# More units of the block-product scheme with tokens on partitions, in a fused attention and mixture-of-experts kernel

## The chip, the cores and the metric

One core of one Trainium2 chip. The metric is the device time of one execution in microseconds; times before and after are medians over runs. The engines are named as the profile names them: PE is TensorE's matmul, PEld its weight load, DVE is VectorE, ACT ScalarE, POOL GpSimd (here it mostly issues loads), SP SyncE, whose queue issues the DMA transposes, the small loads and the stores.

## The reference

Attention with a sliding window of 128 positions and 4 sink positions over 4 batches, 8 heads, 768 tokens and a head size of 64, then a mixture of 4 experts over the 3072 tokens that it gives, where each row is the 8 heads side by side (512 values):

```python
scores = scale * np.matmul(q, k.transpose(0, 1, 3, 2))
keep = is_sink | in_window          # k < n_sink, or 0 <= q - k < window
a = exp(where(keep, scores, -1e9) - max); a = a / sum(a)
x = (a @ v).transpose(0, 2, 1, 3).reshape(3072, 512)
p = domain_probs / domain_probs.sum(-1)
for e in range(4):
    h = np.maximum(x @ w1[e], 0.0)          # 512 -> 1024
    out += p[:, e:e + 1] * (h @ w2[e])      # 1024 -> 512
```

Only matmul inputs are bf16; sums are fp32.

## The kernel before

**Pairs and units.** The tokens are worked in pairs (b, g): batch b, two tiles of 128 tokens (256 tokens), so three pairs to a batch and twelve in all. A unit (b, g, e) is one pair and one expert: its *first products* make the hidden values H (x times w1, ReLU, gate), its *second products* turn H into output rows.

**Two ways of first products.** A plain unit runs 32 matmuls of 256 columns (L1118). A fast unit replaces the 2 by 2 block product by seven products of half the size, P1 to P7 (run in the order P1, P5, P6, P2, P7, P3, P4), over formed sums of the weights and of the tokens. Seven eighths of the columns are left. `START` says from which pair on an expert's units are fast.

**Two ways of fast units.** `emit_fast` (L1208) has F, the hidden index, on partitions: 56 matmuls of 128 columns, 8 to a product, into PSUM tiles `cps`; VectorE does ReLU and gate in one instruction (L1241), with gates spread over all partitions in a tile that a DMA fills (L478). `emit_turning` (L1320), a *turned* unit, has tokens on partitions: 14 matmuls of 512 columns, two to a product, and here a gate is one number per partition (`own_gates`). So the unit's values come out the wrong way round and are turned by two DMA transposes on SP's queue. The steps, in the order of a unit:

- P1: if the PSUM bank of tile Y was not wholly written by such a unit before, a clearing product of 512 columns; ScalarE copies X to Y (seed).
- P5: ScalarE copies it (L1373, `keep`) into `c5`, which is the memory of half-tile X[1], read as fp32.
- P6: VectorE adds c5 and X into V (L1367, `both`); P7 and P3 accumulate onto this.
- P7: VectorE adds into c5 (L1382). P4 ends the unit.
- Gates: ReLU (L1338) and then a scale (L1341) on ScalarE, or both in one on VectorE (L1345), into the bf16 half-tiles X[0] and X[1]; when both halves of one are in, SP issues its transpose into H[:, k] (L1301).

**Half-tiles.** A turned unit opens only when two half-tiles are free. They are not its own: `self.resting` is a list of (time, tile) that starts empty and is filled with memory that other stages have done with (the gate tiles after the last gated unit, three tiles of `qkn` after batch 3 is transposed, later `onat` and `aT`). After its transpose a half-tile goes back to the list. Which unit may be turned is set by `OWN` (the first batch with `own_gates`) and `TURNED_UNITS`; before, all units from batch 2 on but the first four are turned, 20 in all.

```python
def halves(self):
    return sum(x[0] <= t["pe"] + REST for x in self.resting)
```

The planned time at which a half-tile comes back is the end of its transpose on the planner's clock plus `LANDS`.

**Second products** are also in seven products (L1493), with weight forms and with sums S of H made by VectorE (L1434), but for the pairs (0, 0) and (0, 1), which run plain (L1579) and add expert by expert (`emit_second`).

**Attention.** Loads of q, k, v by POOL (L251 `qkn`, L318 `vx`), transposes of q and k by SP (L263 `qkT`), scores (L708, and the sinks' scores L669) on TensorE, exp on ScalarE (L733), a 0/1 mask on VectorE (L727; batch 0 L742; the first group of batch 0 is masked by a matmul that adds a bias), sums and values (L767, L774), reciprocal R (L801), scaling into `onat` (L819 ACT, L812 and L804 DVE), transposes into `xT` (L791), from which the first products read. w1 and w2 of each expert are loaded by POOL (L331, L341).

**What sets the order.** All instructions are emitted once by a planner in Python. It keeps a clock for each engine; `later(engine, ready, slack, run)` puts work for VectorE or ScalarE on a list, which `flush` empties by due time. The main loop picks the next step of TensorE among attention, first products, products of the second stage and plain second products, by the time at which each is ready and by a priority (`DUE`, `LOW_PRODUCT`, `LOW_SECOND`, `SHARE_OF`, `LEAD` and so on). Each engine then runs its list in this order and waits on semaphores where the data is not there. `EXPERTS` gives the order of experts within a pair. `gates_by_row` and `load_gates` fetch the gate tiles, `NGATE` halves of them in a ring. `own_load` and `own_made` fetch and normalise `own_gates` (four small VectorE steps).

Of the kernel before, what the change touches and what calls it, by code (L numbers as in the profile page):

```python
# [16 lines left out]
def kernel(  # L17
# [12 lines left out]
    nc = tc.nc  # L30
# [33 lines left out]
    EXPERTS = {(1, 0): (0, 2, 1, 3), (1, 1): (3, 2, 1, 0), (1, 2): (3, 2, 1, 0), (2, 2): (2, 0, 3, 1), (3, 1): (3, 2, 1, 0)}  # L64
    FIRST = 1
    START = {0: (1, 0), 1: (0, 2), 2: (0, 0), 3: (1, 0)}
    MIX = 6
    SHARE_OF = (1.01, 0.92, 0.96)
    LEAD = (1.01, 0.99)
    DUE = 1.9  # L70
    LOW_PRODUCT = 2.9
    LOW_SECOND = 2.7
    HIGH_PRODUCT = 1.9
    EARLY = -0.01
    MASK = 5000
    GATE = 800
    GATE0 = 300
    FORM = 6000
    TOKEN = 3000
    MARGIN = 500  # L80
    HOLD = 0
    FULL = 7
    STEP0 = 0.03
# [8 lines left out]
    OPEN = 2.5  # L92
    SOON = 34000
    NEARLY = 2
# [5 lines left out]
    ONE = 2  # L100
    HOLDS = 2
    MORE = 2
    BOTH = 1
    PAIR = 0
    OVER = 4
    ALONE = 2.0
    BEHIND = 1500
    CHORES = 3
    BIASED = 1
# [19 lines left out]
    def act(cols, *deps):  # L129
        at = max([t["act"], *deps])  # L130
        t["act"] = at + max(196, 68 + cols / 1.23)
        return at + max(350, 205 + cols / 1.2)

    def dve(cols, *deps, rate=0.96, fixed=157):
        at = max([t["dve"], *deps])
        t["dve"] = at + fixed - 85 + cols / rate
        return at + fixed + 35 + cols / rate

# [23 lines left out]
    def later(engine, ready, slack, run):  # L162

        pend.append((ready, ready + slack, engine, run))
# [294 lines left out]

    gate_sb = {}  # L460
    gate_tiles = [consts.tile([P, 2, 2, P], FP32, name=f"gates{i}") for i in range(NGATE // 2)]
# [21 lines left out]

# [26 lines left out]
    for tb in (2, 3):  # L510
# [18 lines left out]
    LOW = 32768.0  # L529
    low = [lent[:, 5 * P:8 * P], lent[:, 8 * P:12 * P]]  # L530
    nc.vector.tensor_scalar(
        out=low[0].rearrange("p (n q) -> p n q", n=3)[:, 0::2], in0=two, scalar1=LOW, scalar2=-LOW, op0=ALU.mult, op1=ALU.add,
    )
    nc.vector.tensor_scalar(out=low[0][:, P:2 * P], in0=own, scalar1=-LOW, scalar2=None, op0=ALU.mult)
    nc.vector.memset(low[0][0:NSINK, 0:2 * P], 0.0)
# [3 lines left out]
    x = low[1].rearrange("p (n c q) -> p n c q", n=2, c=2)  # L539
    nc.scalar.activation(out=x[:, :, 0], in_=two, func=AF.Copy, scale=-LOW)  # L540
    nc.scalar.activation(out=x[:, :, 1], in_=two, func=AF.Copy, scale=LOW, bias=-LOW)
    mask0 = consts.tile([P, 3 * P], BF16, name="mask0")
    mask1 = consts.tile([P, 4 * P], BF16, name="mask1")
    made = []

    def make_mask(i):
        def run(engine):
            x = (mask0, mask1)[i]
            if i:
                nc.scalar.activation(out=x, in_=low[i], func=AF.Copy, scale=1 / LOW, bias=1.0)  # L550
                act(4 * P)
            else:
                nc.vector.tensor_scalar(out=x, in0=low[i], scalar1=1 / LOW, scalar2=1.0, op0=ALU.mult, op1=ALU.add)
                dve(3 * P)
            made.append(i)
        later(("dve", "act")[i], (24000.0, 11700.0)[i], 8000, run)
# [132 lines left out]
    def scores(b, hp, g, more=False):  # L689
# [10 lines left out]
        if biased:  # L700
            for ph in range(2):
                nc.tensor.matmul(sps[ph][:, 0:w], lhsT=ident, rhs=low[min(g, 1)], start=True, stop=False, skip_group_check=True)
            pe(2 * w, ready, n=2)
# [18 lines left out]
        if b == 0:  # L722
            part = join(2, masked)
        else:
            def mask_both(at):
                def run(engine):
                    nc.vector.tensor_mul(a, a, m[:, None, :].to_broadcast([P, 2, w]))  # L727
                    masked(dve(2 * w, rate=1.92))
                later("dve", at, MASK, run)
            part = join(2, mask_both)  # L730
        for ph in range(2):
            def run(engine, ph=ph):
                nc.scalar.activation(out=a[:, ph], in_=sps[ph][:, 0:w], func=AF.Exp, scale=scale)  # L733
                at = act(w)
                take(slots[ph], at)
                if b or biased:
                    part(at)
                    return
                assert 1 in made

                def mask_one(engine):
                    nc.vector.tensor_mul(a[:, ph], a[:, ph], m)  # L742
# [217 lines left out]
    class Mixture:  # L960


        def __init__(self):
# [61 lines left out]
        def opened(self, b, g, e):  # L1025
# [58 lines left out]
        def emit_first(self, what, ready):  # L1084
# [56 lines left out]
            def run(engine):  # L1141
# [5 lines left out]
                part(at)  # L1147
            later("dve", end, GATE0, run)

# [32 lines left out]
        def emit_fast(self, u, m, ready):  # L1182
# [40 lines left out]
            def gated(dst, src, half_, ready, slack, slot=None, then=None):  # L1223
# [16 lines left out]
                def run(engine):  # L1240
# [5 lines left out]
                    if then:  # L1246
                        then(at)
                later("dve", ready, slack, run)

# [35 lines left out]
        def emit_turning(self, u, m, ready):  # L1285
# [47 lines left out]
            def gated(k, s, src, ready, slack, slot=None, then=None):  # L1333
                gate = own_gates[:, 2 * ((b - OWN) * NG + g) + s, e:e + 1]

                def run(engine):
                    if engine == "act":
                        nc.scalar.activation(out=src, in_=src, func=AF.Relu)  # L1338

                        def scaled(engine):  # L1340
                            nc.scalar.mul(X[k][:, :, s], src, gate)  # L1341
                            done(act(n))
# [3 lines left out]
                    done(dve(n, fixed=OWNED_READ))  # L1346

# [218 lines left out]
        def emit_second(self):  # L1566
# [20 lines left out]
            def run(engine):  # L1587
                if e == 0:
                    nc.vector.tensor_scalar(out=dst, in0=op, scalar1=sc, scalar2=None, op0=ALU.mult)
                else:  # L1590
                    nc.vector.scalar_tensor_tensor(
                        out=dst, in0=op, scalar=sc, in1=dst, op0=ALU.mult, op1=ALU.add,
                    )
# [43 lines left out]
    work = [sum(NFB * NDB * G * (1 if (b, g) < START[e] else 7 / 8) + NFB * NDB * G * (1 if (b, g) < PAIRS[0] else 7 / 8) for g in range(NG) for e in range(E)) for b in range(B)]  # L1637
    ahead, upto, loaded, wide, rowed = 0, 0.0, 0, 0, 0
    asked = []
# [22 lines left out]
    while mix.more() or att.more():  # L1662
# [31 lines left out]
        if turns and (ahead < 2 or not mix.second) and landed.get(("qk", *turns[0]), 1e12) < now and (turns[0][0] <= ahead or turns[0][0] == ahead + 1 and not att.todo):  # L1694
# [17 lines left out]
        if ahead + 1 < B and not att.more() and (ahead == 0 or (ahead + 1, 0) in turned_at) and (ahead == 0 or mix.done >= sum(work[:ahead]) * LEAD[ahead - 1]):  # L1712
            ahead += 1
            if ahead == 1:
                own_load()
            elif ahead == 2:
                own_made()
            att = Attention(ahead)
# [79 lines left out]
```

## Time and profile before

| what | value |
|---|---|
| median of 3 runs | 353.89 us (353.55 to 354.12) |
| span of the profiled execution | 351.9 us |
| PE matmuls L1208 (fast, F on partitions) | 1120 in 20 units |
| PE matmuls L1320 (turned) | 280 in 20 units |
| PE matmuls L1118 (plain) | 256 in 8 units |
| DVE gate L1241 | 72 (54 from cps, 18 from H), 683 ns each |
| ACT ReLU L1338 / scale L1341 | 44 of 585 ns / 37 of 693 ns |
| gate loads L478 on SP | 20 of 128 KB |
| granted TensorE clock | 9 tenths or more in every one of 40 slices |
| POOL busy | 71.6 us, all of it in the first 200 us |

The busy time of PE is the sum over its instructions in the trace; the share in brackets is of the span. PEld, the weight load, overlaps PE. A matmul's own duration in the groups (273 ns for 256 columns) is longer than the spacing of two in a row, since they are pipelined: prices are better read as spacings, and the chain of waits gives these where many of one kind stand in a row. The timeline gives start, duration, engine, line, operation and, in brackets, how long the instruction waited and for whom.

### The profile page before, as it was taken

To read this page: it belongs to the slowest core of one execution; us is meant where nothing else is said; L and a number is where in the kernel's file an instruction comes from. 1 tells how busy PE (TensorE), PEld (TensorE's weight loads), DVE (VectorE), ACT (ScalarE), POOL (GpSimd) and SP (SyncE) were. 2 spreads that over 40 slices of the span, in tenths; PEclk is the share of its full clock that TensorE was granted. 3 is DMA by queue.
4 is the path that set the end of the run, shared out by engine and by line. 5 is a ranking of instruction groups with operands and counts; after the bars stand their busy time and mean duration, and the time that the engine had idled before them with its cause. 6 is when DMAs were issued, how large, how long until landed. Compare 5 with 4: busy or idle time off the path is not lost.

```text
span 351.9 us, 9351 instructions
## 1 busy us (share of the span) xinstructions
PE 346.2 (98%) x3721; PEld 266.0 (76%) x3721; DVE 282.8 (80%) x672; ACT 208.3 (59%) x476; POOL 71.6 (20%) x89
## 2 busy tenths in 40 slices
PE   8999999999999999999999999999999999999996
PEld 3685769656789998998999886755856676666685
DVE  5886999878999999799898999578768586675740
ACT  6863624447874443647453539689589767666611
POOL 8946114330546206100152000000000000000000
PEclk9999999999999999999999999999999999999999
DMA  9999999999999999920999602545437733545441
GB/s 178 178 188 195 223 214 181 179 160 174 162 147 165 121 145 122 132 64 9 109 173 159 113 32 62 120 101 120 80 91 174 127 89 93 120 120 115 67 120 61
DMA packets 161032, 45.61 MB, mean 130 GB/s; under 512 B 144740, under 2 KB 156996, under 8 KB 160988
## 3 DMA queue, kind: packets, MB, share of 16 engines
q0 software_dynamic: 79104, 17.31, 56.4%
q1 hardware_dynamic: 80828, 27.18, 40.1%
q8 instruction: 29, 0.48, 0.5%
q10 hardware_dynamic: 1056, 0.52, 0.5%
q14 instruction: 15, 0.12, 0.1%
HBM read 38.39 MB, written 6.34 MB: 127 GB/s over the span
## 4 chain that ended last, share of the span: by engine, by line
PE 75%; DMA 19%; POOL 5%; issue 1%; ACT 0%; POOLq 0%; SPq 0%
PE acc L1493 35%; PE cps L1320 17%; PE cps L1208 15%; DMA w<-in_moe_w_dram 12%; DMA qkn<-in_k_dram 4%; DMA qkT<-qkn 3%; PE sps L708 3%; PE od L774 2%; POOL qkn L251 2%; POOL w L331 1%; POOL vx L318 1%; PE hps L1118 1%; PE od L767 1%; POOL w L341 0%; PE acc L1579 0%
## 5 line engine op out<-in xcount | busy, mean ns | idle before, releaser
L1493 PEld LDWEIGHTS <-H 128*128 128x128 bf16 x708 | 66.5, 98 | 17.9 <-issue 1.1
L1493 PE MATMUL acc<-w,H 128*128 128x256 bf16 x420 | 56.9, 273 | 0.0
L733 ACT ACTIVATE aT<-sps 128x512 bf16<-128x512 f32 (+1 forms) x96 | 47.2, 579 | 16.3 <-PE sps L708 16.2
L1208 PEld LDWEIGHTS <-w 128*128 128x128 bf16 x640 | 39.1, 98 | 1.2 <-issue 0.5
L1493 PEld LDWEIGHTS <-S 128*128 128x128 bf16 x320 | 30.3, 98 | 9.5 <-issue 0.8
L1241 DVE SCALAR_TENSOR_TENSOR H<-cps,gates 128x512 bf16<-128x512 f32 x54 | 36.6, 683 | 0.0
L1338 ACT ACTIVATE cps<-cps 128x512 f32<-128x512 f32 x44 | 25.5, 585 | 17.5 <-PE cps L1320 17.0
L1118 PE MATMUL hps<-xT,w 128*128 128x256 bf16 x256 | 31.9, 273 | 0.1
L819 ACT ACTIVATE onat<-od,R 128x64 bf16<-128x64 f32 x108 | 24.9, 324 | 11.4 <-DVE R L801 11.1
L318 POOL DMA_DIRECT2D vx<-in_v_dram x24 | 21.4, 903 | 43.0 <-PE od L774 31.2
L1208 PEld LDWEIGHTS <-vf 128*128 128x128 bf16 x480 | 29.3, 98 | 1.0 <-issue 0.5
L1579 PE MATMUL acc<-w,H 128*128 128x512 bf16 x128 | 29.9, 379 | 0.0
L1493 PE MATMUL acc<-wf,H 128*128 128x256 bf16 (+1 forms) x216 | 29.6, 272 | 0.0
L1118 PEld LDWEIGHTS <-w 128*128 128x128 bf16 x256 | 24.1, 98 | 4.7 <-issue 0.9
L1341 ACT ACTIVATE rest<-cps,own_gates 128x512 bf16<-128x512 f32 x37 | 25.5, 693 | 0.7
L727 DVE TENSOR_TENSOR aT<-aT,mask 128x1024 bf16<-128x1024 bf16 (+1 forms) x36 | 22.7, 640 | 3.1 <-ACT aT L733 2.8
L251 POOL DMA_DIRECT2D qkn<-in_q_dram x22 | 19.7, 896 | 23.3 <-DMA qkT<-qkn 14.7
L1208 PE MATMUL cps<-T,w 128*128 128x128 bf16 x320 | 24.3, 219 | 0.0
L1208 PE MATMUL cps<-xT,w 128*128 128x128 bf16 x320 | 24.1, 219 | 0.0
L1320 PE MATMUL cps<-w,T 128*128 128x512 bf16 x80 | 23.8, 379 | 0.0
L1320 PE MATMUL cps<-vf,T 128*128 128x512 bf16 x80 | 23.6, 379 | 0.0
L1554 ACT COPY osb<-acc 128x256 f32<-128x256 f32 x32 | 12.1, 382 | 19.3 <-PE acc L1493 19.1
(145 smaller groups left out, 673.5 us busy)
## 6 DMA issues: line engine op xcount, KB each, us to landing
w<-in_moe_w_dram POOLq DMA_DIRECT2D x6, 1024.0 KB, 18.4
out_dram<-osb SPq DMA_DIRECT2D x16, 256.0 KB
vx<-in_v_dram POOLq DMA_DIRECT2D x24, 128.0 KB, 6.5
qkn<-in_q_dram POOLq DMA_DIRECT2D x22, 128.0 KB, 6.7
qkn<-in_k_dram POOLq DMA_DIRECT2D x22, 128.0 KB, 7.4
gates<-gate_rows SPq DMA_DIRECT2D x20, 128.0 KB
w<-in_moe_w_dram POOLq DMA_DIRECT2D x4, 256.0 KB, 6.9
w<-in_moe_w_dram POOLq DMA_DIRECT2D x2, 512.0 KB, 11.5
```

The lines of the kernel that those rows point to most:

```text
L251: nc.gpsimd.dma_start(out=both[:, i], in_=src[b, :, tb * P:(tb + 1) * P, :].rearrange("h p d -> p h d"),)
L318: nc.gpsimd.dma_start(out=vx[tb][:, :, 0:D], in_=v[b, :, tb * P:(tb + 1) * P, :].rearrange("h p d -> p h d"),)
L733: nc.scalar.activation(out=a[:, ph], in_=sps[ph][:, 0:w], func=AF.Exp, scale=scale)
L819: nc.scalar.mul(o[:, qi, hp, ph * D:(ph + 1) * D], od[:, qi, ph, 0:D], R[:, qi, ph])
L1118: nc.tensor.matmul(h[:, i].rearrange("p (q n) -> p q n", q=2), lhsT=w1_sb[e][:, db, fb * P:(fb + 1) * P], rhs=xT[b, g][:, :, db], start=(i ...
L1208: nc.tensor.matmul(y[:, f], lhsT=A[:, d, f * P:(f + 1) * P], rhs=T[:, d], start=(m in ("P1", "P5") and f == 0 and d == 0), stop=(d == 1), ...
L1241: nc.vector.scalar_tensor_tensor(out=dst, in0=src, scalar=0.0, in1=gate, op0=ALU.max, op1=ALU.mult)
L1320: nc.tensor.matmul(y.rearrange("p f n -> p (f n)"), lhsT=T[:, d], rhs=A[:, d], start=(m in ("P1", "P5") and d == 0), stop=(d == 1), skip_g ...
L1338: nc.scalar.activation(out=src, in_=src, func=AF.Relu)
L1341: nc.scalar.mul(X[k][:, :, s], src, gate)
L1493: nc.tensor.matmul(y, lhsT=self.operand(b, g, e, m)[:, f], rhs=forms[e][m][:, f, cs], start=(k == 0 and f == 0 and m in (("P1", "P5", "P2" ...
L1579: nc.tensor.matmul(op, lhsT=H[:, fb // QF, fb % QF, s], rhs=w2_sb[e][:, fb, :], start=(fb == 0), stop=(fb == NFB - 1),)
```

## The change

Sizes and switches:

```diff
-        [(0, 0, 2), (1, 1, 1)],
+        [(1, 1, 1), (0, 0, 2)],
...
-    NGATE = 4
+    NGATE = 2
     TURN_ABOUT = 1
-    OWN = 2
-    TURNED_UNITS = (4, 0)
-    EXPERTS = {(1, 0): (0, 2, 1, 3), (1, 1): (3, 2, 1, 0), ...}
+    OWN = 1
+    TURNED_UNITS = (1, 0, 1, 0, 0, 1, 1, 0, 1, 1, 1, 0, 1, 1, 1, 0, 1, 1, 1, 1, 1, 1, 0, 1, 1, 1, 1, 1, 1, 1, 1, 1, 1, 1, 1, 1)
+    EXPERTS = {(1, 0): (0, 2, 3, 1), (1, 1): (0, 3, 2, 1), ...}
...
-    START = {0: (1, 0), 1: (0, 2), 2: (0, 0), 3: (1, 0)}
+    START = {0: (1, 0), 1: (0, 2), 2: (0, 0), 3: (0, 2)}
...
-    REST = 3000
-    LANDS = 0
-    SCALED = 300
+    REST = 4000
+    LANDS = -1400
+    SCALED = 1100
...
-    OWNED_READ = 152
+    OWNED_READ = 218
+    OWNS = 9000
+    HALVES = 2
+    GATE_LANDS = 600
```

`TURNED_UNITS` is now one 0 or 1 for each unit from batch `OWN` on, in the order in which units are opened: 7 units of batch 1, 10 of batch 2 and 12 of batch 3 are turned, 29 instead of 20. With `START` one more unit, (0, 2, 3), is fast instead of plain. `own_gates` holds 18 tiles of tokens instead of 12. Some thirty other numbers of the planner (`MIX`, `SHARE_OF`, `LEAD`, `LOW_SECOND`, `EARLY`, `MASK`, `FORM`, `MARGIN`, `SOON`, `BEHIND` and the like, and the costs in `act` and `dve`) are set anew, so the order of instructions moves on every engine.

Half-tiles: two tiles of their own stand on the list from the start; after batch 3 is transposed the three of `qkn` are added as before.

```diff
-            self.turning = set(mine[TURNED_UNITS[0]:len(mine) - TURNED_UNITS[1]])
+            self.turning = {u for u, x in zip(mine, TURNED_UNITS) if x}
...
-            self.G, self.resting = {}, []
+            self.G = {}
+            self.resting = [(0.0, mo.tile([P, QF, 2, P], BF16, name=f"row{i}", tag=f"row{i}", bufs=1)) for i in range(HALVES)]
...
-                    if not TURNED_UNITS[1] and self.gated[-1] == (b, g, e):
+                    if self.gated[-1] == (b, g, e):
                         self.rest_gates()
```

Gates: with a ring of one tile (two halves) a load has to wait for the unit before the last; the planner now knows when a gate tile lands (`gate_at`), and a gate is planned no earlier.

```diff
-        sp(takes=300)
+        gate_at[pair, e] = sp(takes=300) + GATE_LANDS
...
-            later("dve", end, GATE0, run)
+            later("dve", max(end, gate_at[b * NG + g, e]), GATE0, run)
```

Masks: two tiles (384 and 512 columns) become two overlapping views of one of 512; the multiply of the four-run groups reads it as four runs of 256.

```diff
-    mask0 = consts.tile([P, 3 * P], BF16, name="mask0")
-    mask1 = consts.tile([P, 4 * P], BF16, name="mask1")
+    masks = consts.tile([P, 4 * P], BF16, name="masks")
+    mask0, mask1 = masks[:, P:], masks[:, 0:2 * P]
...
-                    nc.vector.tensor_mul(a, a, m[:, None, :].to_broadcast([P, 2, w]))
+                    x = a if g == 0 else a.rearrange("p h (r c) -> p (h r) c", r=2)
+                    nc.vector.tensor_mul(x, x, m[:, None, :].to_broadcast([P, 2 if g == 0 else 4, w if g == 0 else 2 * P]))
```

In `emit_second` the first expert's scaling moves from VectorE to ScalarE, and `own_made` is issued `OWNS` after `own_load` on the planner's clock instead of at the start of batch 2:

```diff
                 if e == 0:
-                    nc.vector.tensor_scalar(out=dst, in0=op, scalar1=sc, scalar2=None, op0=ALU.mult)
-                else:
...
+                    nc.scalar.mul(dst, op, sc)
+                    acc_free[bank] = act(Dout)
+                    return
...
-            later("dve", end, 400, run)
+            later("dve" if e else "act", end, 400, run)
...
+        if owned + OWNS < now:
+            owned = 1e12
+            own_made()
```

The planned cost of the scale on ScalarE and of the gate on VectorE is set higher (`act(n + 125)`, and a rate and a fixed part for the one in `c5`), and the first masks' making is rearranged (ScalarE makes half of the tile in two instructions of 128 columns, VectorE the other half).

More of the change, by code (lines that the diff above doesn't have):

```diff
@@ L58 @@
     ]
-    NGATE = 4
+    NGATE = 2
     TURN_ABOUT = 1
-    OWN = 2
-    TURNED_UNITS = (4, 0)
-    EXPERTS = {(1, 0): (0, 2, 1, 3), (1, 1): (3, 2, 1, 0), (1, 2): (3, 2, 1, 0), (2, 2): (2, 0, 3, 1), (3, 1): (3, 2, 1, 0)}
+    OWN = 1
+    TURNED_UNITS = (1, 0, 1, 0, 0, 1, 1, 0, 1, 1, 1, 0, 1, 1, 1, 0, 1, 1, 1, 1, 1, 1, 0, 1, 1, 1, 1, 1, 1, 1, 1, 1, 1, 1, 1, 1)
+    EXPERTS = {(1, 0): (0, 2, 3, 1), (1, 1): (0, 3, 2, 1), (1, 2): (3, 0, 2, 1), (2, 2): (2, 1, 0, 3), (3, 1): (1, 3, 0, 2), (3, 2): (0, 1, 3, 2), (2, 0): (2, 0, 3, 1), (0, 2): (0, 1, 3, 2), (3, 0): (3, 2, 0, 1), (2, 1): (2, 3, 1, 0), (0, 1): (1, 2, 3, 0)}
     FIRST = 1
-    START = {0: (1, 0), 1: (0, 2), 2: (0, 0), 3: (1, 0)}
-    MIX = 6
-    SHARE_OF = (1.01, 0.92, 0.96)
-    LEAD = (1.01, 0.99)
+    START = {0: (1, 0), 1: (0, 2), 2: (0, 0), 3: (0, 2)}
+    MIX = 9
+    SHARE_OF = (1.1, 1.01, 0.95)
+    LEAD = (0.995, 1.02)
     DUE = 1.9
     LOW_PRODUCT = 2.9
[L72 to L76, printed above, removed]
+    LOW_SECOND = 2.4
+    HIGH_PRODUCT = 2.0
+    EARLY = -0.3
+    MASK = 9000
+    GATE = 2000
     GATE0 = 300
-    FORM = 6000
-    TOKEN = 3000
-    MARGIN = 500
+    FORM = 4000
+    TOKEN = 1000
+    MARGIN = 600
     HOLD = 0
     FULL = 7
-    STEP0 = 0.03
+    STEP0 = 0.28
     READY = 40
-    REST = 3000
-    LANDS = 0
-    SCALED = 300
+    REST = 4000
+    LANDS = -1400
+    SCALED = 1100
     SHARED = 2
     MARGIN1, MARGIN2 = 4000, 14000
-    OWNED_READ = 152
+    OWNED_READ = 218
+    OWNS = 9000
+    HALVES = 2
+    GATE_LANDS = 600
     WIDE = 2
-    OPEN = 2.5
-    SOON = 34000
+    OPEN = 1.8
+    SOON = 28000
     NEARLY = 2
@@ L100 @@
     ONE = 2
-    HOLDS = 2
+    HOLDS = 3
     MORE = 2
@@ L104 @@
     PAIR = 0
[L105 to L108, printed above, removed]
+    OVER = 6
+    ALONE = 2.5
+    BEHIND = 1900
+    CHORES = 2
     BIASED = 1
@@ L130, in act @@
         at = max([t["act"], *deps])
-        t["act"] = at + max(196, 68 + cols / 1.23)
-        return at + max(350, 205 + cols / 1.2)
+        t["act"] = at + max(200, 76 + cols / 1.23)
+        return at + max(375, 230 + cols / 1.2)
     def dve(cols, *deps, rate=0.96, fixed=157):
         at = max([t["dve"], *deps])
-        t["dve"] = at + fixed - 85 + cols / rate
-        return at + fixed + 35 + cols / rate
+        t["dve"] = at + fixed - 77 + cols / rate
+        return at + fixed + 60 + cols / rate
     def pool(cols, *deps, fixed=190):
@@ L529 @@
     LOW = 32768.0
-    low = [lent[:, 5 * P:8 * P], lent[:, 8 * P:12 * P]]
+    low = lent[:, 5 * P:8 * P]
     nc.vector.tensor_scalar(
-        out=low[0].rearrange("p (n q) -> p n q", n=3)[:, 0::2], in0=two, scalar1=LOW, scalar2=-LOW, op0=ALU.mult, op1=ALU.add,
+        out=low.rearrange("p (n q) -> p n q", n=3)[:, 0:2], in0=two, scalar1=LOW, scalar2=-LOW, op0=ALU.mult, op1=ALU.add,
     )
-    nc.vector.tensor_scalar(out=low[0][:, P:2 * P], in0=own, scalar1=-LOW, scalar2=None, op0=ALU.mult)
-    nc.vector.memset(low[0][0:NSINK, 0:2 * P], 0.0)
+    nc.vector.tensor_scalar(out=low[:, 2 * P:], in0=own, scalar1=-LOW, scalar2=None, op0=ALU.mult)
+    nc.vector.memset(low[0:NSINK, P:], 0.0)
     nc.vector.reduce_sum(
@@ L547, in run @@
         def run(engine):
-            x = (mask0, mask1)[i]
             if i:
-                nc.scalar.activation(out=x, in_=low[i], func=AF.Copy, scale=1 / LOW, bias=1.0)
-                act(4 * P)
-            else:
-                nc.vector.tensor_scalar(out=x, in0=low[i], scalar1=1 / LOW, scalar2=1.0, op0=ALU.mult, op1=ALU.add)
-                dve(3 * P)
+                nc.scalar.activation(out=masks[:, 0:P], in_=own, func=AF.Copy, scale=-1.0, bias=1.0)
+                nc.scalar.copy(out=masks[:, P:2 * P], in_=own)
+                act(P)
+                act(P)
+            else:
+                nc.vector.tensor_scalar(out=masks[:, 2 * P:], in0=low[:, P:], scalar1=1 / LOW, scalar2=1.0, op0=ALU.mult, op1=ALU.add)
+                dve(2 * P)
             made.append(i)
@@ L701, in scores @@
             for ph in range(2):
-                nc.tensor.matmul(sps[ph][:, 0:w], lhsT=ident, rhs=low[min(g, 1)], start=True, stop=False, skip_group_check=True)
+                nc.tensor.matmul(sps[ph][:, 0:w], lhsT=ident, rhs=low, start=True, stop=False, skip_group_check=True)
             pe(2 * w, ready, n=2)
@@ L1247, in run @@
                         then(at)
-                later("dve", ready, slack, run)
+                later("dve", max(ready, gate_at[b * NG + g, e]), slack, run)
             if m == "P1":
@@ L1345, in run @@
                     nc.vector.tensor_scalar(out=X[k][:, :, s], in0=src, scalar1=0.0, scalar2=gate, op0=ALU.max, op1=ALU.mult)
-                    done(dve(n, fixed=OWNED_READ))
+                    done(dve(n, fixed=OWNED_READ) if slot is not None else dve(n, rate=1.92, fixed=214))
                 def done(at):
@@ L1637 @@
     work = [sum(NFB * NDB * G * (1 if (b, g) < START[e] else 7 / 8) + NFB * NDB * G * (1 if (b, g) < PAIRS[0] else 7 / 8) for g in range(NG) for e in range(E)) for b in range(B)]
-    ahead, upto, loaded, wide, rowed = 0, 0.0, 0, 0, 0
+    ahead, upto, loaded, wide, rowed, owned = 0, 0.0, 0, 0, 0, 1e12
     asked = []
@@ L1715 @@
                 own_load()
-            elif ahead == 2:
-                own_made()
+                owned = now
             att = Attention(ahead)
```

16 lines of the change are left out of this document (7 added, 9 removed).

## The prediction

> **What bounds the kernel now.** I read the engine totals first, then the view of waits for the matmul engine alone, then the chain of waits in order of time, and last the timeline where a turned unit ends.
>
> ```profile
> PE 346.2 (98%) x3721; PEld 266.0 (76%) x3721; DVE 282.8 (80%) x672; ACT 208.3 (59%) x476; POOL 71.6 (20%) x89
> ```
>
> ```profile
> PE acc L584 <- DVE lent L489: 1.4, 1, 1.4
> PE sinks L669 <- DMA qkT<-qkn: 0.3, 1, 0.3
> PE tx L838 <- DVE onat L804: 0.2, 1, 0.2
> ```
>
> TensorE is busy 346.2 of 351.9 us, and the second view is all of its visible waiting: 1.4 us before the first matmul, 0.3 us for the transposed q and k of batch 1, 0.2 us near the start. A modelled end can hide a short stall, so I also summed, over the trace, the spacing of matmul starts beyond columns/2.4 GHz plus 2.4 ns: 3.3 us are lost in the first 20 us, 0.5 us at 85 us, and nothing worth naming after. So the kernel can gain only by less TensorE work or a better start, while any new wait of TensorE is paid in full.
>
> ```profile
> 75.11 10.75 DMA qkT<-qkn
> ...
> 95.75 1.75 PE hps L1118 x16
> ...
> 119.19 3.57 PE cps L1208 x64
> ...
> 228.34 3.03 PE cps L1320 x14
> ```
>
> These lines of the chain (start, us, what) give the prices: 1.75/16 = 109 ns for a plain matmul of 256 columns (L1118), 3.57/64 = 55.8 ns for one of 128 (L1208), 3.03/14 = 216.4 ns for one of 512 (L1320). The first line is a DMA transpose issued while loads were running: 10.75 us until its reader could go on.
>
> ```profile
> 328.65 0.58 ACT L1373 COPY rest<-cps 128x512 f32<-128x512 f32 x1 [0.30 <-PE cps L1320]
> ...
> 329.90 0.69 DVE L1367 TENSOR_TENSOR cps<-rest,cps 128x512 f32<-128x512 f32 x1
> ...
> 332.56 0.58 ACT L1338 ACTIVATE cps<-cps 128x512 f32<-128x512 f32 x1 [0.38 <-PE cps L1320]
> ...
> 333.18 0.69 ACT L1341 ACTIVATE rest<-cps,own_gates 128x512 bf16<-128x512 f32 x1
> ```
>
> ```profile
> 333.89 2.58 SPq L1301 DMA_TRANSPOSE H<-rest  x2
> ...
> 338.12 0.42 DVE L1434 TENSOR_TENSOR S<-H 128x512 bf16<-128x512 bf16 x1 [2.76 <-DMA H<-rest]
> ```
>
> This is a turned unit in the timeline. ScalarE copies P5 into the half-tile (L1373), VectorE adds it to P6 (L1367) and frees P7; after P4 ScalarE does ReLU (L1338) and gate (L1341), and the sync queue issues the transposes 0.02 us later. Two are issued 1.33 us apart; the reader of the second starts 2.90 us after its issue (335.22 to 338.12), with quiet DMA.
>
> **The change, part by part.** *TensorE work.* In the instruction lists L1208 goes from 20 units to 12, L1320 from 20 to 29, L1118 from 8 to 7. 448 matmuls less at 55.8 ns are -25.0 us, 126 more at 216.4 ns are +27.3, 32 less at 109.4 ns are -3.5; one more clearing product of 512 columns (+0.22), one more filler of 256 (+0.11), one more turn to 64-row scores (+0.1: 12 such matmuls take 0.55 us behind others, 0.44 in a run). Together -0.8 us.
>
> [...]
>
> *The 0.3 us wait at 85 us.* The sinks product that waits for qkT stands 0.3 us later in the new TensorE order, and the loads ahead of it are in the same order, so some -0.3 us (0 to -0.46).
>
> *VectorE and ScalarE.* VectorE loses 52 gate multiplies of about 0.68 us and gets 22 of 0.49 to 0.75 and 18 additions of 0.69: about -12 us. ScalarE gets 14 more L1338 (0.58), 14 more L1341 (0.69), 10 more copies: about +17 us, in stages where it is busy 13 to 17 of 30 us. Neither moves the end by its sum, since no wait on them is seen now; if the cover goes, it shows in the waits priced below. The masks read from one tile handle the same elements (0.55 and 0.69 us at L727, before), the first multiply of a second product goes to ScalarE four times, the order in the first score group is only swapped: nothing, hidden behind matmuls; bounds -0.3 to +0.3 us in the start. A gate ring of two halves lets a gate load start only when the unit before the last is finished; 20 gate loads become 11, and each next gated unit begins over 4 us after its load can be issued (a load took 3 to 8 us): nothing, at worst 1 us once.
>
> *The sync queue.* 18 more transposes of 1.23 us issue are 22 us of a queue that mostly waits. Behind them stand xT and qkT transposes and stores. The shortest way from the last values of a group to the first use of its xT shrinks from 26.7 to 15.8 us in batch 1: still covered.
>
> *The half-tiles: the new wait.* Until batch 3 has turned its qkT only two tiles, row0 and row1, hold turned units, so each unit overwrites what the unit before is still having transposed. The copy L1373 must wait for that transpose; behind it stand, in order, all of ScalarE, then L1367 on VectorE, then P7 and P3. I counted matmul time (columns/2.4 GHz + 2.4 ns) from the last product of one owner to the P5 of the next. Before: 4.24 us at least, then 4.67. After: 2.63 and 2.09 us in two neighbouring units, then 4.14 and more.
>
> First pair (matmul time 147 to 152): P4 ends at 147.29, and ScalarE's list has a copy of acc between ReLU and gate; that waits for a product ending at 148.17. So +0.20 (end of a product to ScalarE, as at 332.56), 0.30 for the copy, gate 148.67 to 149.36, issue 149.38, reader 2.90 later at 152.28, copy 0.59, addition 0.03 + 0.69, hand-over 0.1: P7 can start at 153.7; its turn is 151.92. **+1.8 us.** Second pair: P3 of the owner ends at 152.78, +0.20, ReLU and gate 1.3: first transpose at 154.3, the second 1.25 behind it, reader at 158.45, +1.4: P7 at 159.85 instead of 158.78. **+1.1 us.** Bounds: 0 for each if the gates end earlier than I set them; a loaded queue adds (10.75 against 2.9).
>
> *Turned units amid loads.* No row shows an H transpose there.
>
> ```profile
> 100.83 4.47 SPq L263 DMA_TRANSPOSE qkT<-qkn  x2
> ```
>
> ```profile
> 108.38 0.88 POOL L251 DMA_DIRECT2D qkn<-in_q_dram  x1 [6.56 <-DMA qkT<-qkn]
> ```
>
> The trace's completions put the landing of the first of these at 107.56: 6.7 us, behind seven loads and beside two more; others took 5.2 to 10.2. In the new order two places meet a burst of loads. The first use of unit (1,0,3) comes 6.3 us after its transpose can be issued: 0 (quiet) to +3.9 (10.2 us); by the 6.7 us row, which has nearly that load ahead, **+0.4**. At matmul time 188 the copy's P7 would wait 1.4 us if the transpose takes the 5.4 us of the xT issued at 170.09 behind two loads, nothing if quiet, 5.6 at 9.7 us; I take half of the row, **+0.7**, since the third load is issued only as it starts.
>
> *Sum.* -0.8 - 0.3 + 1.8 + 1.1 + 0.4 + 0.7 = +2.9 us on the profiled 351.9 us. That execution lies 2.0 us under the median of the runs, 353.89 us, so I forecast 356.8 us. 0.2% (0.7 us) is about what a measurement of this kernel can tell from no change.
>
> **The rivals.** *The matmul sum stands* (352.8 us): -1.1 us and no wait. The deciding point is whether the half-tile is free 1.4 us ahead of P7: the transpose must land by 150.5 and 157.3 in matmul time, 3.2 us after P4 ended. For it: the present program's own reuse (4.24 us) shows no ScalarE wait on a landing, and any idle of TensorE in between widens the gap. Against: gate and landing alone take 0.20 + 1.3 + 2.9 = 4.4 us on the measured rows. 0.24. [...]
>
> *Break-even* (353.9 us): the waits cost just what the matmuls save, because the acc copy comes early and one pair is covered (1.1 us left). 0.11.
>
> *The loads starve the transposes* (360 us): both crowded places at 9.7 us instead of 6.7 and half of 5.4: 3.4 + 5.6 in place of 1.1, less what one stall gives the other; I take half of the 7.9 more, +4. For it: 9.5 to 10.2 us was measured for four transposes between 111 and 122 us, while ten loads were under way. Against: nine loads, and two of them wait themselves. 0.15.
>
> *That the change does not do what it says*: the lists show 29 turned units and 7 of batch 1, so no chance is kept.
>
> **How the numbers follow.** Half-tile waits 0.50 (354.7 to 358.5 us), starving 0.15, break-even 0.11, matmul sum 0.24. Slower 0.65, same 0.11, faster 0.24. The range 352.6 to 360.2 us holds the matmul sum, the forecast and most of the starving; the likeliest case alone is 354.7 to 358.5.
>
> **What would show it.** L1377 (L1373 today) waiting on DMA of H<-row by some 2 us twice, near 152 and 160 us; then TensorE waiting on VectorE at P7 by 1.8 and 1.1 us, where it now waits on nothing. A first wait on H near 128 us and one near 195 us. TensorE's matmul sum down by 0.8 us. If TensorE shows no wait over 0.3 us after 20 us, I am wrong on the half-tiles; if the waits stand elsewhere, on the place.

## The result, and the profile after

| what | before | after |
|---|---|---|
| median of 6 runs, us | 353.82 (353.55 to 354.12) | 383.25 (377.51 to 384.62) |
| ratio to before | 1 | 1.075 (95% interval 1.071 to 1.080) |
| profiled span, us | 351.9 | 381.3 |

The kernel's median is 29.4 us longer, and so is the profiled span, which the rest of this part accounts for. The ratio compares fast runs alone: after the change the three longest runs (383.44 to 384.62 us) count as slow, and the other three have a median of 380.8 us, 27.0 us above before. First the line of totals of the page, and its line of granted clock in 40 slices:

```profile
PE 352.9 (93%) x3369; PEld 253.5 (66%) x3369; DVE 274.9 (72%) x660; ACT 223.9 (59%) x494; POOL 72.4 (19%) x89
...
PEclk9999999999999989899999879999999999999999
```

There are 352 matmuls fewer. Priced by the prediction's formula, which fits the spacings of the trace before (medians of 56, 109 and 216 ns in rows of matmuls of 128, 256 and 512 columns, so 2.4 ns and 0.417 ns a column), they come to 345.46 us against 346.41. Yet the busy time of PE has grown by 6.7 us, and the clock is below full in four slices. The waiting of TensorE that the trace names, but for two waits of 0.2 us, with its totals, times and longest:

```profile
PE cps L1324 <- DVE cps L1371: 12.2, 5, 6.8
PE sps L709 <- ACT onat L822: 3.6, 1, 3.6
PE acc L1497 <- DMA H<-row: 3.5, 1, 3.5
PE od L770 <- ACT rest L1345: 2.1, 1, 2.1
PE cps L1212 <- DVE cps L1265: 1.5, 3, 1.0
PE acc L585 <- DVE lent L492: 1.4, 1, 1.4
```

Of these only the last stood in the profile before. The chain of waits (start, us, what) shows what is behind four of the others:

```profile
123.97 10.32 DMA H<-row
...
144.52 8.70 DMA H<-row
...
166.06 3.11 DMA H<-row
...
174.36 4.89 DMA H<-row
...
208.06 9.80 DMA H<-row
...
263.83 3.23 DMA H<-rest
```

These are transposes of turned units, from issue to the reader. The reader is a different one each time. For the one issued at 208 us it is the copy of the next unit's P5 into the half-tile that is being transposed (timeline: start, us, engine, line):

```profile
206.24 1.73 SPq L794 DMA_TRANSPOSE xT<-onat  x1
208.06 3.10 SPq L1305 DMA_TRANSPOSE H<-row  x1
...
217.94 0.59 ACT L1377 COPY row<-cps 128x512 f32<-128x512 f32 x1 [7.33 <-DMA H<-row]
...
218.56 0.69 DVE L1371 TENSOR_TENSOR cps<-row,cps 128x512 f32<-128x512 f32 x1 [10.24 <-ACT row L1377]
...
219.31 1.01 PE L1324 MATMUL cps<-w,T 128*128 128x512 bf16 x2 [6.75 <-DVE cps L1371]
```

For the one issued at 144 us it is a sum S for the second products on VectorE, and behind it in VectorE's order stands the attention of another batch:

```profile
153.31 0.42 DVE L1438 TENSOR_TENSOR S<-H 128x512 bf16<-128x512 bf16 x1 [5.21 <-DMA H<-row]
...
153.99 0.17 DVE L804 RECIPROCAL R<-od 128x4 f32<-128x4 f32 x1
...
154.20 0.93 ACT L822 ACTIVATE onat<-od,R 128x64 bf16<-128x64 f32 x4 [5.58 <-DVE R L804]
...
155.18 1.10 PE L709 MATMUL sps<-qkT 64*128 64x128 bf16 x11 [3.56 <-ACT onat L822]
```

Read upwards: the scores wait for a PSUM bank, that for ScalarE's scaling, that for a reciprocal of 0.17 us, and that for a sum of a unit it has nothing to do with. The 1.5 us at L1212 begin the same way, with a load that was issued at 38.71 us and took 19.2 us:

```profile
57.95 0.23 DVE L1625 TENSOR_REDUCE own_sum<-own_gates 128x18 f32<-128x72 f32 x1 [1.59 <-DMA own_gates<-in_moe_domain_probs_dram]
```

The clock is read from the table by stretches (us, PE busy, ..., then PEclk, DMA share, GB/s):

```profile
127.82:131.23 3.41, 3.00 (x37) 2.37 (x34) 3.41 (x8) 0.94 (x2) 0.00 (x0) 1.00 1.95 167
131.23:134.64 3.41, 0.31 (x3) 0.29 (x4) 1.37 (x3) 0.00 (x0) 0.00 (x0) 1.00 1.65 121
134.64:138.05 3.41, 3.41 (x20) 2.40 (x19) 0.67 (x2) 0.70 (x2) 0.00 (x0) 0.50 1.63 221
138.05:141.46 3.41, 3.41 (x27) 2.36 (x25) 2.79 (x9) 1.42 (x4) 0.00 (x0) 1.00 0.89 186
```

After the stall at 130.6 us TensorE runs at half clock for 3.41 us: matmuls of 256 columns stand 213 ns apart there, against a median of 109 in this trace. It is busy in all of that window, so this costs 1.7 us on top of the stall. The same follows the stalls at 151 us (one window) and 212 us (two in a row, most of the first of them idle). The trace thus accounts for the loss as follows, with gaps between matmul starts for the stalls:

| place, us | what TensorE waits behind | us |
|---|---|---|
| 130.6 | second product, H of (1,0,3), landing 10.3 us after issue | 3.7 |
| 151.4 | VectorE's sum, H of (1,1,3), 8.7 | 3.7 |
| 168.5 | copy of P5 of (1,2,3), half-tile of (1,1,2), 3.1 | 2.1 |
| 177.4 | copy of P5 of (1,2,0), half-tile of (1,2,3), 4.9 | 3.2 |
| 212.3 | copy of P5 of (2,0,0), half-tile of (2,0,2), 9.8 | 6.9 |
| 266.0 | copy of P5 of (2,2,1), half-tile of (2,1,0), 3.2 | 2.3 |
| 58 to 61 | VectorE, load of own_gates | 1.6 |
| four windows | half clock | 5.0 |
| | gaps under 0.5 us, the rest | 2.3 |
| | matmuls (-0.95) and the wait for qkT at 85 us (-0.46) | -1.4 |
| | sum | 29.4 |

### The profile page after: what moved, and what is told of

Same layout as the page of the kernel before. It is cut to its first block, busy times and chain, and to the rows that moved or that the text cites. A ratio compares the mean times of both kernels' runs of the same rounds, so it can differ in the third digit from the quotient of the medians.

```text
span 381.3 us, 8694 instructions
## 1 busy us (share of the span) xinstructions
PE 352.9 (93%) x3369; PEld 253.5 (66%) x3369; DVE 274.9 (72%) x660; ACT 223.9 (59%) x494; POOL 72.4 (19%) x89
## 4 chain that ended last, share of the span: by engine, by line
PE 69%; DMA 19%; DVE 7%; ACT 2%; issue 1%; POOL 0%; ACTq 0%; POOLq 0%; DVEq 0%; SPq 0%
PE acc L1497 27%; PE cps L1324 19%; DMA H<-row 12%; PE cps L1212 7%; PE acc L1583 5%; DMA own_gates<-in_moe_domain_probs_dram 5%; PE hps L1122 3%; PE sps L709 2%; PE od L777 2%; DMA vx<-in_v_dram 2%; DVE cps L1371 1%; ACT row L1377 1%; DMA H<-rest 1%; DVE aT L745 1%; DVE row L1349 1%
## 5 line engine op out<-in xcount | busy, mean ns | idle before, releaser
L1324 PE MATMUL cps<-w,T 128*128 128x512 bf16 x116 | 35.3, 386 | 12.2 <-DVE cps L1371 12.2
L1324 PEld LDWEIGHTS <-T 128*128 128x128 bf16 x232 | 22.0, 99 | 23.2 <-issue 13.8
L1324 PE MATMUL cps<-vf,T 128*128 128x512 bf16 x116 | 34.6, 386 | 0.0
L1324 PE MATMUL cps<-w,xT 128*128 128x512 bf16 x116 | 34.5, 383 | 0.0
L1212 PEld LDWEIGHTS <-w 128*128 128x128 bf16 x384 | 24.6, 99 | 5.6 <-issue 2.3
L729 DVE TENSOR_TENSOR aT<-aT,masks 128x1024 bf16<-128x1024 bf16 (+1 forms) x36 | 22.7, 642 | 5.0 <-ACT aT L735 4.9
L1364 ACT COPY cps<-cps 128x512 f32<-128x512 f32 x29 | 16.9, 581 | 11.6 <-PE cps L1324 11.3
L1122 PEld LDWEIGHTS <-w 128*128 128x128 bf16 x224 | 21.2, 98 | 3.6 <-issue 0.2
L1345 ACT ACTIVATE row<-cps,own_gates 128x512 bf16<-128x512 f32 x33 | 23.1, 699 | 0.5
L1438 DVE TENSOR_TENSOR S<-H 128x512 bf16<-128x512 bf16 x35 | 14.3, 419 | 12.6 <-DMA H<-row 10.2
L1324 PEld LDWEIGHTS <-xT 128*128 128x128 bf16 x174 | 16.5, 99 | 9.4 <-issue 0.6
## 6 DMA issues: line engine op xcount, KB each, us to landing
w<-in_moe_w_dram POOLq DMA_DIRECT2D x2, 512.0 KB, 11.6
```

What stands on the lines that cost most here:

```text
L729: nc.vector.tensor_mul(x, x, m[:, None, :].to_broadcast([P, 2 if g == 0 else 4, w if g == 0 else 2 * P]))
L1122: nc.tensor.matmul(h[:, i].rearrange("p (q n) -> p q n", q=2), lhsT=w1_sb[e][:, db, fb * P:(fb + 1) * P], rhs=xT[b, g][:, :, db], start=(i ...
L1212: nc.tensor.matmul(y[:, f], lhsT=A[:, d, f * P:(f + 1) * P], rhs=T[:, d], start=(m in ("P1", "P5") and f == 0 and d == 0), stop=(d == 1), ...
L1324: nc.tensor.matmul(y.rearrange("p f n -> p (f n)"), lhsT=T[:, d], rhs=A[:, d], start=(m in ("P1", "P5") and d == 0), stop=(d == 1), skip_g ...
L1364: nc.scalar.copy(out=tiles["Y"], in_=y)
```

## The experiments

Theory A: the loss is late landings (A1: slow under loads; A2: too close to the reuse of a half-tile, also when quiet), and the half clock that follows. Rival B: the refitted order. The first four runs share a chip; the kernel before took 353.79 us beside them.

**The turned units of batch 1 put back.**

```diff
-    TURNED_UNITS = (1, 0, 1, 0, 0, 1, 1, 0, 1, 1, 1, 0, 1, 1, 1, 0, ...)
+    TURNED_UNITS = (0, 0, 0, 0, 0, 0, 0, 0, 0, 0, 0, 0, 1, 1, 1, 0, ...)
```

> The 7 units of batch 1 run with F on partitions again (12 zeros at the head of the mask), the 22 of batches 2 and 3 stay turned, all else as changed. Theory A (TensorE loses its time to late landings of the transposes of turned units, and to a halved clock after each stall of over 3.4 us): the four stalls of 3.7, 3.7, 2.1 and 3.2 us before 180 us go, and two half-clock windows of 3.4 us with them (1.7 us each); the stall at 212 us stays. 383.3 - 12.7 - 3.4 + 0.6 (seven units by 0.09 us of matmuls) = 368 us, between 360 and 372, as the order shifts. Rival B (the refitted constants put attention and second products in a worse order, the turned units are not the cause): 378 us or more.

358.89 us, ratio 1.016 (1.012 to 1.019). Far below B's number, and 1 us below A's range too: the planner orders anew, and in its new order the stall at 212 us, which A had kept, is gone as well. Of the 44 transposes of turned units one took over 5 us (6.1), and the clock was full throughout. B's bound of 378 us is broken.

**The 20 units of before.**

```diff
+    TURNED_UNITS = (0, 0, 0, 0, 0, 0, 0, 0, 0, 0, 0, 0, 0, 0, 0, 0, 1, 1, 1, 1, ...)
```

> The mask names the 20 units that were turned before (the last 20 of batches 2 and 3), with the two half-tiles of their own, the gate ring of two, the one mask tile and all refitted constants kept. Theory A: the stalls in batch 1 and the one at 212 us go, since the first turned unit starts later and the half-tiles get three more partners in batch 3: 353 to 360 us. Rival B: 370 us or more.

358.61 us, ratio 1.014 (1.013 to 1.016). The time is in the range of theory A, with 4.8 us left over though no more units are turned than before: VectorE waits 1.4 us for own_gates and 1.4 us for gate loads, one copy still meets a landing (0.8 us on TensorE), and the rest is in gaps of 0.1 to 0.5 us. What the refitted order adds to these by itself is not separated here.

**Lighter loads, same order.**

```diff
+            if b >= 2:
+                flat = src.rearrange("b h s d -> (b h s d)")[(6 * b + tb) * P * H * D:(6 * b + tb + 1) * P * H * D]
+                nc.gpsimd.dma_start(out=both[:, i].rearrange("p h d -> p (h d)"), in_=flat.rearrange("(p n) -> p n", p=P))
...
-                out=vx[tb][:, :, 0:D],
+                out=vx[tb][:, 0:n, 0:D],      # n = 1 from batch 2 on
```

> Same order of all instructions as the changed kernel; the loads of q and k of batches 2 and 3 read the same number of bytes as rows of 2 KB from other places (8 times fewer packets), those of v read one head of eight. Theory A1 (the long landings of 8.7 to 11.6 us come from the loads under way): transposes that took 10.3, 8.7 and 9.8 us take 3 to 5; the stalls of 3.7, 3.7 and 6.9 us shrink to under 1.5 us each, their half-clock windows (5.4 us) go, the stalls of 2.1, 3.2 and 2.2 us on a reused half-tile stay: 383.3 - 14.3 + 2 - 5.4 = 366 us, between 362 and 370. Rival (the transposes are slow because SP's queue or the half-tiles hold them up): 378 us or more, and landings of over 8 us remain.

372.67 us, ratio 1.053 (1.049 to 1.057): between the two. The stall at 130 us is gone, those at 151 and 212 us are 1.9 and 4.7. But transposes of 6.2 to 9.0 us remain, so these loads were not light enough to decide it.

**No credit for half-tiles.**

```diff
-    REST = 4000
+    REST = 0
```

> REST 4000 -> 0: a turned unit is opened only when its half-tiles are planned free at that time, not up to 4 us later; nothing else is edited, the planner orders anew. Theory A2 (part of the loss is the 4 us of credit that lets the copy of P5 meet a half-tile still in transposing): no wait of that copy on a landing in quiet stages (2.1, 3.2, 2.2 us go); but with only two half-tiles the units open later, other work has to fill in, and where there is none TensorE waits all the same: 365 to 380 us. If the two half-tiles are no limit: 360 us or less. If the credit does no harm: 380 us or more.

380.3 us, ratio 1.074 (1.071 to 1.077): no gain, on the number set for "the credit does no harm", but not because nothing changed. The copy meets a landing once (3.8 us) instead of six times, but now the sums on VectorE do (17.9 us, five times) and TensorE idles 4.8, 4.2 and 4.1 us. With two half-tiles the wait moves rather than goes.

**A third half-tile, same order** (before beside it and the next three: 353.87 us).

```diff
-            self.resting = [(0.0, mo.tile(..., name=f"row{i}", ...)) for i in range(HALVES)]
+            self.free = [mo.tile(..., name=f"row{i}", ...) for i in range(HALVES + 1)]
+            self.resting = [(0.0, None)] * HALVES
...
-    gate_tiles = [consts.tile([P, 2, 2, P], FP32, name=f"gates{i}") for i in range(NGATE // 2)]
+    gate_tiles = [None] * (NGATE // 2)
...
-                self.G[b, g, e] = [self.half(), self.half()]
+                self.G[b, g, e] = [self.half(), self.half()][::-1]
```

> Same order of instructions as the changed kernel, but the half-tiles are handed out from three pieces of memory in turn instead of two, the one longest free for X[1], into which P5 is copied. The memory is that of the gate tile: the 11 gate loads are left out and the gate multiplies of the units with F on partitions read the mask tile. Theory A2 (the copy of P5 meets a half-tile still being transposed): no wait of that copy on a landing between 160 and 270 us; the stalls of TensorE of 2.1, 3.2, 6.9 and 2.2 us there and one double half-clock window (2.0 us) go, those at 130 and 151 us (3.7 each) and their half-clock windows (1.7 each) stay: 383.3 - 14.4 - 2.0 = 367 us, between 364 and 371. Rival (late landings stop the sums on VectorE and the second products just as much, the half-tile is only where it shows first): 375 us or more.

370.48 us, ratio 1.049 (1.045 to 1.054), in theory A's range. The stalls at 168, 177 and 266 us are gone, as expected, and ScalarE waits for no landing of an H. The one at 212 us is 3.7 us and stands behind a sum on VectorE instead: a late landing that no longer stops the copy stops the next reader.

**Third half-tile and lighter loads.**

> The third piece of memory for half-tiles (gate loads left out) and the light loads of q, k, v of batches 2 and 3 together, order unchanged. Theory A (loads and half-tiles are the whole of the loss): only the stalls on the sums of batch 1 (1.9 us with light loads) and on own_gates (1.6 us) stay, no half-clock window beyond one: the order's own 347.8 us by the planner, 3.1 us of tail and 2.0 us around the span, plus 3.5 to 5: 355 to 359 us. Rival (something else in the refitted order costs as much): 363 us or more.

365.8 us, ratio 1.032 (1.025 to 1.039): missed, on the rival's side. Its trace keeps two transposes of 11.0 and 10.8 us at 136 us, right beside the light loads, and a stall of 5.8 us behind them.

**own_gates later, with the 20 units of before.**

```diff
-    OWNS = 9000
+    OWNS = 20000
```

> The 20 units that were turned before, as in the run of the old mask, and OWNS 9000 -> 20000, so that VectorE's first step on own_gates is issued 11 us later. Theory: VectorE no longer waits 1.4 us for the load of own_gates at 57 us and TensorE not the 1.5 us behind it: 358.6 - 1.5 = 357.1 us, between 356.5 and 357.8. Rival (VectorE is late there anyway): 358.3 us or more.

359.58 us, ratio 1.017 (1.014 to 1.019): missed. The wait for own_gates is gone, but in the new order VectorE waits 2.4 us for one gate load.

**The gate ring alone, in the kernel before.**

```diff
-    NGATE = 4
+    NGATE = 2
```

> The kernel before with one edit, NGATE 4 -> 2: a ring of two halves for the gates. The prediction set this at nothing, at worst 1 us: 353.8 to 354.8 us. Rival (with two halves each gate load is issued only when the unit before the last is done, and VectorE waits for it unit after unit): 357 us or more.

Four runs from 358.24 to 363.66 us; over the three shorter ones the ratio is 1.019 (1.012 to 1.027): 4 to 9 us for an edit that the prediction set at nothing. SP's queue and VectorE in its timeline:

```profile
122.00 9.45 SPq L263 DMA_TRANSPOSE qkT<-qkn  x2
131.96 1.47 SPq L478 DMA_DIRECT2D gates<-gate_rows  x2
...
135.63 0.69 DVE L1241 SCALAR_TENSOR_TENSOR H<-cps,gates 128x512 bf16<-128x512 f32 x1 [5.67 <-DMA gates<-gate_rows]
```

In this execution a transpose at the head of SP's queue waits for a load of q and k that lands at 130.2 us, and the gate load stands behind it. TensorE then stops 5.5 us, and 6.8 us of half clock follow. The profiled run is the longest of the four (363.66 us), so these are the lengths of a bad case; the others were not traced.

**No loads in batches 2 and 3** (before beside both: 354.00 us).

```diff
+            if b >= 2:
+                nc.gpsimd.memset(both[:, i], 0.0)
+            else:
+                nc.gpsimd.dma_start(...)
...
+            if b < 2:
+                nc.gpsimd.dma_start(out=vx[tb][:, :, 0:D], ...)
```

> Order of the changed kernel; the loads of q, k and v of batches 2 and 3 are left out (GpSimd clears the q and k tiles instead, v keeps batch 1's values), so after 115 us only stores, gate loads and transposes are left to the DMA. The light loads left landings of 7 to 11 us, so they were no clean test. Theory A1 (loads under way make the transposes late): every transpose of a turned unit after 120 us lands in 3.0 to 5 us; the stalls at 130 us (3.7) and 151 us (3.7) go, the one at 212 us falls from 6.9 to 1 to 3, those of 2.1, 3.2 and 2.2 us on a reused half-tile and 1.6 us behind own_gates stay, no half-clock window: 383.3 - 7.4 - 5 - 5.4 = 365.5 us, between 362 and 368. Rival (the transposes hold up one another and SP's queue, loads or not): landings of over 7 us remain, 370 us or more.

368.86 us, ratio 1.042 (1.041 to 1.044), 1 us over the expected range. No transpose of a turned unit takes over 5.0 us, and the stalls at 130 and 151 us are gone. What is left of TensorE's waiting is the half-tiles, and own_gates:

```profile
PE cps L1328 <- DVE cps L1375: 8.1, 4, 3.1
PE od L774 <- ACT rest L1349: 2.2, 1, 2.2
PE cps L1216 <- DVE cps L1269: 1.6, 2, 1.3
```

I had expected no half-clock window. There were two, after stalls of only 2.9 and 2.3 us.

**Third half-tile and no loads.**

> The third piece of memory for half-tiles (gate loads left out, gates read from the mask tile) and no loads of q, k, v of batches 2 and 3, order unchanged. Theory A (late landings under loads and half-tiles reused too soon are the whole loss): no stall over 1 us after 20 us; the order's matmuls of 345.4 us, 4 to 5 us lost in the start and in small gaps, 3 us of tail and 2 us around the span: 354 to 357 us. Rival (something else in the refitted order): 360 us or more.

354.92 us, ratio 1.003 (1.002 to 1.004), as theory A expected. All of TensorE's waits:

```profile
PE acc L585 <- DVE lent L492: 1.4, 1, 1.4
PE cps L1215 <- DVE cps L1268: 0.7, 1, 0.7
PE cps L1328 <- DVE row L1390: 0.6, 1, 0.6
PE od L777 <- DMA vx<-in_v_dram: 0.3, 1, 0.3
PE tx L841 <- DVE onat L807: 0.2, 1, 0.2
```

The order of matmuls is that of the changed kernel, so that order can run at the speed of the kernel before once these two are out of its way: the profiled span is 353.1 us against 381.3, and 28.2 of the 29.4 us go with the loads and the short supply of half-tiles, the half clock among them. Alone, the third half-tile takes 14.3 us off the span and the loads 13.8. (The gate loads are also left out here, which the trace of the changed kernel shows no wait on.)

**An order made for late landings.** The planner of the changed kernel can be told: it takes a quiet landing as 3.03 us (`LANDS` -1400), measured 3.2, but one under loads as 3.4 to 6.4 where the four latest were measured at 8.7 to 11.6, and it doesn't count the copy's wait for a half-tile at all.

```diff
+                            if t["sw"] > t["sp"] - 1000:
+                                done += LOADED        # 4500
...
-                at["P5"] = self.T_at[b, g]
+                at["P5"] = max(self.T_at[b, g], self.F[b, g, e][1])
...
```

> As the 24-unit version, another result of the same fit: 26 units turned (4 of batch 1, 11 of batch 2, 11 of batch 3); its planner ends at 348.4 us. Theory A: 351 to 356 us, a little more exposed to loads than with 24. Rival: 357 us or more.

> The changed kernel with a planner that counts what the runs showed: the landing of a turned unit's transpose 4.5 us later while loads are still under way on its clock, P5 not before the half-tile of its copy is planned free, the gate into the other half not before that one is; the mask, the order of experts and the priorities fitted anew to that planner (24 units turned: 3 of batch 1, 9 of batch 2, 12 of batch 3; two half-tiles and the gate ring of two kept). Its own clock ends at 348.3 us; that of the kernel before ended at 351.2 and its span was 351.9. Theory A (the loss is late landings that the planner did not count): no stall of TensorE over 2 us behind a transpose, 351 to 355 us. Rival (landings under loads vary too much for any plan with this little slack): stalls of 2 to 5 us again in places, 357 us or more.

370.23 us, ratio 1.047 (1.044 to 1.049), with 26 units; 373.61 us with 24, whose order makes some of the output differ for a reason that is open, so that its time is read only beside the other. Both missed, on the rival's side. The 24-unit kernel's longest stall, 8.2 us at 82 us, is not behind a transpose: VectorE waits 10.8 us for a store of the output. The timeline of the 26-unit kernel, at its longest stall:

```profile
235.52 15.96 SPq L795 DMA_TRANSPOSE xT<-onat  x2
...
252.19 2.65 SPq L1310 DMA_TRANSPOSE qkT<-row  x2
...
255.44 1.03 PE L1504 MATMUL acc<-w,qkT 128*128 128x256 bf16 x4 [5.27 <-DMA qkT<-row]
```

No loads of q, k or v run here; the last was issued at 185 us. The second xT transpose is issued at 250.24 us only, right after TensorE's last read of that buffer by the look of the times, and the unit's transposes, whose gates were done at 245.75 us, stand behind it on SP. Transposes of up to 11.4 us came back at 147 us. Its other stalls of over 1 us are 2.3 us behind the load of own_gates, 1.7 behind an xT transpose, and 2.1 and 1.9 behind late H of turned units. Telling the planner of loads and half-tiles moved part of the loss to waits that it does not count and left part of it; whether a fuller plan would do is not shown. No version with more turned units beat the kernel before.

## Why the prediction was wrong, point by point

- **What bounds it**: right. TensorE had no slack, and each new wait was paid in full, and more than in full.
- **Matmul sum**: -0.8 forecast, -0.95 measured. The wait at 85 us went, as forecast.
- **VectorE and ScalarE totals**: -12 and +17 forecast, -7.9 and +15.6 measured; neither set the end.
- **Half-tiles, the two neighbouring units**: right in mechanism and place, +1.8 and +1.1 forecast, 2.1 and 3.2 measured. The second was mis-sized: its transpose took 4.9 instead of 2.9 us (below, last section). The count of gaps named 2.63, 2.09 and then 4.14 us as the shortest; a gap of 3.37 us further on was left out, and it is the 2.3 us at 266.
- **Turned units amid loads**: the step that failed. It gave +0.4 and +0.7 us, from landings of 6.7 and half of 5.4 us; measured were 10.3 and 9.8 us and stalls of 3.7 and 6.9. The mechanism was named, also as a rival at 360 us, but priced by the row of one transpose with seven loads ahead, of which I took the lower end each time. The rival's own two stalls, 3.4 and 5.6 us, were near; I halved what they add and gave them 0.15. The trace of before had no H transpose over 4.4 us for a plain reason: its first one is issued at 215.67 us, after the last load. That was readable, and it says that no row of an H transpose prices the changed place; nearer were the rows of q and k transposes amid loads, 10.75 us in the prediction's own first line of the chain and 10.2 us at 121.57 us. (The prediction counts four transposes of 9.5 to 10.2 us beside ten loads there; the trace has three, issued at 111.59, 115.68 and 121.57 us, and nine loads.)
- **Not in the sum at all**: the sum on VectorE at 151 us (3.7). I followed a late landing to TensorE's first read and to the half-tile, not to the sums (L1438) that read H in VectorE's fixed order ahead of the attention of the next group. Nor the half clock (5.0): a stall was priced at its length. Nor own_gates (1.6).
- **Gate ring**: "nothing, at worst 1 us once". In the changed kernel no wait on gates is seen; in the kernel before the edit alone costs 4 to 9 us. The step held by luck of the order, not for the reason given: in the run of that edit the lead of 4 us is lost once the load stands behind a transpose on SP, and VectorE waits 5.67 us for it.
- **The likeliest case** (356.8 us) and the range (to 360.2) were too low. They counted four places and no half clock, where six places, the queues behind them and the clock add up.

## What to carry to other kernels

A step that turns an on-chip hand-over into a DMA is priced by its landing at the place where it will run, not by the quiet landing, and each reader of the result is followed down its engine's fixed order: here a wait of VectorE of 5.2 us on one unit's H held up another batch's attention, and TensorE by 3.7 us. Before a moved transfer is costed from a trace, look whether any transfer of its kind ran beside the same loads; if none did, the row gives no upper bound: here no H transpose of before took over 4.4 us, and after the change the latest took 8.7 to 11.6. Where TensorE is busy to 98%, as before the change, a stall is priced at its length and at what half clock may follow: here the stalls at 130, 151 and 212 us took 14.3 us, and the half clock behind them 5.0.

## What the runs showed of the hardware

**Half clock after a stall.** In the changed kernel's trace the granted clock changes at points that lie 3.41 us or a whole multiple of it apart. Laid in stretches of 3.41 us from these points, the three at full clock in which PE was busy for 0.31, 0.00 and 0.00 us (from 131.2, 151.7 and 213.1 us) were each followed by one at half clock, and the one at half clock with 0.66 us (216.6 us) by another. Those at full clock with 1.55, 2.06, 1.69 and 1.96 us (168.8, 175.6, 179.0 and 264.3 us) were followed by full clock; the stalls there, of 2.1, 3.2 and 2.3 us, each reach over two stretches. Two rows of the run without loads, by such stretches:

```profile
250.73:254.14 3.41, 1.28 (x18) 1.00 (x18) 1.85 (x7) 1.48 (x3) 0.00 (x0) 1.00 0.43 85
254.14:257.55 3.41, 3.41 (x21) 2.00 (x20) 1.91 (x7) 2.21 (x7) 0.00 (x0) 0.50 0.52 102
```

The stall is 2.3 us and lies inside one stretch. In the same run a stretch with PE busy for 1.48 us (from 165.4 us) was followed by full clock. So one stall of 2.3 us was followed by half clock, and one of 3.2 us was not: the "stall of over 3.4 us" of theory A fits the changed kernel (3.7, 3.7 and 6.9 us), not the run without loads (2.9 and 2.3 us). These are single cases; where the limit lies, and whether there is a fixed one, is not shown.

**Quiet transposes that landed late.** The transpose at 174.36 us took 4.89 us; its last part landed at 4.89, the parts before it at 3.34. In its flight the trace's packets show one of 16 KB on the queue named instruction, for 0.92 us. Three other quiet transposes with such a packet in flight took 4.4 to 4.6 us (226.6, 242.0 and 273.4 us), but others with one took no more than 3.0 to 4.1 (297.1 and 228.0 us); those without took 3.0 to 3.6. That is a correlation; no run took these packets away.

**A quiet transpose took longer in the changed kernel**: from 224 us on, median 3.2 us from issue to landing, against 2.75 in the profile before. The cause is open.
